# A turned tile of maxima takes its PSUM bank from another of two lists

## The chip, the cores and the metric

The kernel runs on one core of a Trainium2 chip. The metric is device time in microseconds (us); lower is better. The kernel before was run three times without the profiler: 1486.66, 1487.3 and 1488.96 us, median 1487.3. One further execution was profiled, and all rows quoted below come from that one.

## The reference

One transformer layer in its parallel form, float32, on 2048 rows of width 512: a layer norm, then attention with 32 heads of width 16 and a two-layer MLP of width 1792, both on the same normalised rows, and both added to the input.

```python
xn = _layernorm(x)
qkv = (xn @ wqkv).reshape(B, S, 3, H, Dh).transpose(2, 0, 3, 1, 4)      # S 2048, H 32, Dh 16
scores = jnp.einsum("bhqd,bhkd->bhqk", q, k) * Dh ** -0.5
p = jax.nn.softmax(scores, axis=-1)
o = jnp.einsum("bhqk,bhkd->bhqd", p, v).transpose(...).reshape(B, S, D) @ wo
h = jax.nn.gelu(jnp.einsum("bsd,df->bsf", xn, w1) + b1, approximate=True)
out = x + o + jnp.einsum("bsf,fd->bsd", h, w2) + b2
```

The softmax needs the largest score of each row before it can take exponents, and that maximum is where the change sits.

## The kernel before

**Blocks and units.** Attention is cut into 32 blocks (`t`): 8 groups of four heads times 4 stretches of 512 queries. A block has 16 units, so there are 512 units (`u`). In the unit loop (`unit`, line 745) two blocks are in work at once. Unit `u` computes the scores S of block `u // 16` for their maxima, four products of 128 queries by 512 keys, one for each head (`s_half`, line 366); VectorE (DVE) takes a row maximum of each (line 363, the tile `mt`). Unit `u` also computes, for `e = u - 19`, the transposed scores T (keys by queries; `e_half`, line 399), with the negative maximum already inside as extra rows of the operand `qst`, and ScalarE (ACT) takes the exponent of each (line 410, the tile `pe`). TensorE (PE) then multiplies the exponents by the values into a bank V (`v_half`, line 413).

**The order in a unit.** A unit has two slots, `a = 0` and `a = 1`. Written out, PE does: S of head 0, T of head 1, S of head 1, T of head 0, then a stretch of V products and of D products; then S of head 2, T of head 3, S of head 3, T of head 2, and V and D again. Below these are called S0, T1, S1, T0, S2, T3, S3, T2, and those of the next unit S0', T1' and so on. Each product is four matmuls of 32 columns, and uses one half (64 rows) of the PE array; S0 and T1, or V and D, run side by side in the two halves. "D" is all the other matrix work of the layer (projections, MLP, output projection), cut into groups and threaded through the units (`dense`, line 686): two to four products in a slot, by the group's pace. The order on every engine is the order in which the code is written; no scheduler changes it.

**The banks.** PSUM has eight banks, and four lists of them: S with banks 0, 1, 2; T with 3, 4, 5; D with 6; V with 7 (line 102). `banks(tag)` (line 107) takes the bank at the head of a list and puts it at the tail at once, so with three banks a product gets the bank that the product three before it in its list had. The matmul that first writes a bank waits until the last reader of that bank is done: a DVE maximum for an S bank, an ACT exponent for a T bank. When a D group ends, its bank goes to the tail of T's list and the next D group takes the head of that list (`dbank`, line 513; `Group.end`, line 550), so the T list always holds three banks while a D group is open, but one of the three may be a bank that D had until then. The finish of a D group reads it once, on ACT for most groups.

**The turn of the maxima.** After the last unit of a block, `s_end` (line 372) reduces `mt` to the block's negative maxima `mneg` (line 379) and leaves a closure `store` behind. It runs in the first unit of the next block, between the slots (line 783): two small matmuls by the identity turn `mneg` into a bank (line 386), DVE splits the turned tile into two float16 parts `mhl` (lines 389 and 390), and two DMAs write them out (line 393), from where four small DMAs (`m_rows`, line 345) bring them into the rows of `qst` that the block's T products read, three units later. There are 31 such turns in the unit loop, at units 32, 48, ..., 512; the turn of the first block is in the planned part before the loop, and has a bank of its own there.

Which reader the turn and the products behind it wait for follows from the lists. In 24 of the 31 turns no D group ended in the slot just before. In the other seven (units 64, 128, 256, 304, 336, 432 and 512) one did, and its bank has just gone to the tail of T's list.

Of the kernel before, what the change touches and what calls it, by code (L numbers as in the profile page):

```python
# [19 lines left out]
S = 2048  # L20
# [34 lines left out]
def layer_kernel(ctx: ExitStack, tc: tile.TileContext, x, wqkv, wo, w1, b1, w2, b2, out):  # L55
# [48 lines left out]
    def bank_tile(k, tag):  # L104
        return ps.tile([P, QB], F32, tag=f"B{k}", bufs=1, name="p" + tag)

    def banks(tag):
        k = free_banks[tag].pop(0)
        free_banks[tag].append(k)
        return bank_tile(k, tag)  # L110
# [48 lines left out]
    def given(engine, ns):  # L159
        backlog[engine] += ns  # L160
# [180 lines left out]
    def m_rows(t, h):  # L341
        g, qb = divmod(t, NQB)
        p, a = divmod(h, 2)
        dst = qst[g % 2][qb][64 * a + 62:64 * a + 64, p].rearrange("r (t q) -> r t q", q=P)
        nc.sync.dma_start(dst, m_d[t, 4 * h:4 * h + 4].rearrange("t r q -> r t q"))
# [26 lines left out]
    def s_end(u):  # L372

        t, i = divmod(u, 16)
        if i < 15:
            return
        g, qb = divmod(t, NQB)
        mneg = mnegs[t % 2]
        nc.vector.tensor_reduce(mneg[:, :16], mt_of[t].rearrange("p h t k -> p (h t) k"), axis=AX.X, op=ALU.max, negate=True)
        given("dve", 220)  # L380

        def store():

            pt = banks("S")
            for a in range(2):
                nc.tensor.matmul(pt[32 * a:32 * a + 32, :64], mneg[64 * a:64 * a + 64, :],
                                 ident[64 * a:64 * a + 64, 64 * a:64 * a + 64], start=True, stop=True)
            mhl = work.tile([64, 2, 64], F16, name="mhl", bufs=2)
            nc.vector.tensor_scalar_mul(mhl[:, 0], pt[:64, :64], 1.0 / MROW)
            nc.vector.scalar_tensor_tensor(mhl[:, 1], pt[:64, :64], 1.0 / MROW, mhl[:, 0], op0=ALU.mult, op1=ALU.subtract)  # L390
            given("dve", 300)
            for a in range(2):
                nc.sync.dma_start(m_d[t, :, :, 64 * a:64 * a + 64], mhl[32 * a:32 * a + 16])
            for h in range(4):
                m_rows(t, h)

        stores[t] = store
# [1097 lines left out]
```

## Time and profile before

| | |
|---|---|
| median of three runs | 1487.3 us |
| the profiled execution's own time | 1485.57 us |
| its span, first to last instruction | 1483.8 us |
| mean granted PE clock | 0.997 |
| turns of the maxima in the unit loop | 31, the first at 131.5 us, the last at 1415.1 us |

The profiled execution lies 1.7 us under the median of the runs, and 1.77 us of its time lie outside its span. In the rows, "pS", "pT", "pD" and "pV" are banks of the four lists, "gap" and "idle before" are idle time of the engine, and "62*32" names the part of the PE array in use. Rows of a timeline give start in us, length in us, engine, line, operation, tiles, and how many instructions were put together in the row; where several are put together, the length is from the start of the first to the end of the last. Ends of matmuls are modelled, so waits of PE are read from starts.

### The profile page before, as it was taken

Reading aid. Unit: us, or ns where it says so; the run is one execution under the profiler, and the core shown is the slowest. Engines: PE = TensorE matmul, PEld = TensorE weight load, DVE = VectorE, ACT = ScalarE, POOL = GpSimd, SP = SyncE. Lnnn points to the kernel's source line nnn. Section 1 sums busy time; section 2 is a strip of 40 time slices with the busy share of each in tenths; the row PEclk is TensorE's granted clock in tenths of the full one; section 3 lists DMA queues with packets and bytes.
Section 4 is the critical chain, followed back from the end, with each engine's and each line's share of the span. In section 5 each row is a group of like instructions: output and inputs, shape, how many; then the busy total and the mean of one; then the engine's idle time right before and its main releaser. Section 6 shows DMA issues by size and latency. Waiting matters only on the chain.

```text
span 1483.8 us, 88118 instructions
## 1 busy us (share of the span) xinstructions
PE 1467.1 (99%) x40158; PEld 811.5 (55%) x40158; DVE 1374.5 (93%) x2305; ACT 1259.2 (85%) x2366; POOL 662.2 (45%) x672
## 2 busy tenths in 40 slices
PE   8999999999999999999999999999999999999998
PEld 4445555555555555555555555555555555555554
DVE  7889999999999999999999999999999999999923
ACT  5868888888999888899988889998888998888884
POOL 3202857563787301377831037782115777121100
PEclk9999999999999999999999999999999999999999
DMA  6732556554224210221112111121112110111432
GB/s 213 226 113 70 163 171 195 160 157 144 76 72 114 65 37 23 68 62 41 44 43 87 30 36 44 53 73 44 43 38 80 50 37 21 56 55 31 141 93 95
DMA packets 112623, 124.83 MB, mean 84 GB/s; under 512 B 22908, under 2 KB 84220, under 8 KB 112248
## 3 DMA queue, kind: packets, MB, share of 16 engines
q1 hardware_dynamic: 112248, 119.18, 26.6%
q8 instruction: 314, 5.14, 1.5%
q14 instruction: 61, 0.50, 0.1%
HBM read 81.66 MB, written 37.34 MB: 80 GB/s over the span
## 4 chain that ended last, share of the span: by engine, by line
PE 89%; DVE 8%; ACT 1%; DMA 1%; issue 0%; SPq 0%; DVEq 0%; ACTq 0%
PE pV L169 26%; PE pD L169 25%; PE pS L169 18%; PE pT L169 18%; DVE mt L363 7%; PE pT L992 2%; DMA wq<-in_A_wqkv_dram 1%; PE pD L992 0%; DVE ac L1370 0%; ACT xs L945 0%; PE pT L962 0%; ACT xt L966 0%; DVE xt L975 0%; SPq L858 0%; DVE wvh L1075 0%
## 5 line engine op out<-in xcount | busy, mean ns | idle before, releaser
L363 DVE TENSOR_REDUCE mt<-pS 128x1 f32<-128x512 f32 x2029 | 1296.9, 684 | 44.0 <-PE pS L169 24.3
L410 ACT ACTIVATE pe<-pT 128x512 f32<-128x512 f32 x2048 | 1111.5, 599 | 178.0 <-PE pT L169 84.4
L169 PE MATMUL pV<-pe,vv 64*32 64x512 f32 x8192 | 1072.3, 594 | 0.1
L169 PE MATMUL pT<-qst,kst 64*32 64x512 f16 x8192 | 709.8, 378 | 0.5 <-issue 0.5
L169 PE MATMUL pS<-kst,qst 62*32 62x512 f16 x8116 | 614.3, 378 | 3.6 <-DVE mt L363 2.2
L169 PEld LDWEIGHTS <-qst 62*32 62x32 f16 x8192 | 283.6, 92 | 237.5 <-issue 58.0
L169 PE MATMUL pD<-xb,wc 64*32 64x512 f16 x5376 | 360.9, 377 | 0.0
L169 PEld LDWEIGHTS <-kst 64*32 64x32 f16 x8192 | 269.8, 91 | 159.9 <-issue 69.2
L169 PE MATMUL pD<-w_s,g 64*32 64x512 f16 x5376 | 356.4, 377 | 0.0
L169 PEld LDWEIGHTS pV<-pe,vv 64*32 64x32 f32 x8192 | 182.0, 105 | 88.9 <-PE pV L169 4.5
L169 PE MATMUL pD<-xt,wqk_h 64*32 64x512 f16 x2400 | 157.8, 378 | 0.0
L169 PEld LDWEIGHTS <-wc 64*32 64x32 f16 x5376 | 117.0, 91 | 43.0 <-issue 0.6
L169 PEld LDWEIGHTS <-g 64*32 64x32 f16 x5376 | 113.8, 92 | 41.0
L1337 POOL TENSOR_TENSOR xa<-xa,yt 128x512 f32<-128x512 f32 x16 | 20.4, 1278 | 232.0 <-ACT yt L1335 232.0
L466 POOL TENSOR_TENSOR osb<-osb,rb 128x512 f32<-128x512 f32 x31 | 39.8, 1283 | 165.8 <-DMA rb<-den_d 123.4
L1289 POOL TENSOR_TENSOR t<-hh 128x512 f32<-128x512 f32 x56 | 58.2, 1040 | 86.3 <-ACT hh L1312 85.3
L1291 POOL TENSOR_TENSOR t<-t,hh 128x512 f32<-128x512 f32 x56 | 71.7, 1281 | 4.7
L1284 POOL TENSOR_TENSOR t<-t,hh 128x512 f32<-128x512 f32 x56 | 71.7, 1281 | 4.7
L1283 POOL TENSOR_SCALAR t<-t,gs 128x512 f32<-128x512 f32 x56 | 38.7, 692 | 66.0 <-ACT t L1278 66.0
L1286 POOL TENSOR_TENSOR g<-t,g 128x512 f16<-128x512 f32 x56 | 65.2, 1163 | 4.7
L169 PEld LDWEIGHTS <-wqk_h 64*32 64x32 f16 x2400 | 54.5, 92 | 19.4 <-issue 1.4
L169 PE MATMUL pD<-wo_s,oc 64*32 64x512 f16 x828 | 54.7, 378 | 0.0
(160 smaller groups left out, 874.8 us busy)
## 6 DMA issues: line engine op xcount, KB each, us to landing
wc<-w_d SPq DMA_DIRECT2D x56, 256.0 KB
qk_d<-stg SPq DMA_DIRECT2D x32, 256.0 KB
rb<-den_d SPq DMA_DIRECT2D x124, 64.0 KB
wch<-in_B_w_dram SPq DMA_DIRECT2D x14, 512.0 KB
wch<-in_B_w_dram SPq DMA_DIRECT2D x28, 256.0 KB
w_d<-wsp SPq DMA_DIRECT2D x28, 256.0 KB
kst<-qk_d SPq DMA_DIRECT2D x64, 96.0 KB
qst<-qk_d SPq DMA_DIRECT2D x64, 96.0 KB
```

The costliest lines, as they stand in the source:

```text
L169: p = nc.tensor.matmul(*args, **kw)
L363: nc.vector.reduce_max(mt_of[t][:, n, qt, kb:kb + 1], s, axis=AX.X)
L410: nc.scalar.activation(pe, st, AF.Exp, scale=scale_of[g // 2])
L466: pooled((1280, lambda: nc.gpsimd.tensor_tensor(osb, osb, rb, op=ALU.mult)), (620, lambda: nc.gpsimd.tensor_scalar(ot[:, 0], osb, 1.0, 0.0 ...
L992: nc.tensor.matmul(tl[key], lhs, rhs, start=c + n == 0, stop=(c, n) == (NC - 1, 2))
L1283: pooled((690, lambda: nc.gpsimd.tensor_scalar(t1, t1, 1.0, gs[:, 1:2], op0=ALU.add, op1=ALU.mult)), (1280, lambda: nc.gpsimd.tensor_tenso ...
L1284: (1280, lambda: nc.gpsimd.tensor_tensor(t1, t1, hh, op=ALU.mult)),
L1286: (1160, lambda: nc.gpsimd.tensor_tensor(g[:, 1, f, :], t1, g[:, 0, f, :], op=ALU.subtract)),
L1289: pooled((1040, lambda: nc.gpsimd.tensor_tensor(t1, hh, hh, op=ALU.mult)), (620, lambda: nc.gpsimd.tensor_scalar(t1, t1, 1.0, 1.0 / GELU_A ...
L1291: (1280, lambda: nc.gpsimd.tensor_tensor(t1, t1, hh, op=ALU.mult)),
L1337: add = lambda: nc.gpsimd.tensor_tensor(xa, xa, yt, op=ALU.add)
```

## The change

The turn's tile is taken from the list T in place of the list S. Nothing else is edited.

```diff
@@ -381,7 +381,7 @@
 
         def store():
 
-            pt = banks("S")
+            pt = banks("T")
             for a in range(2):
                 nc.tensor.matmul(pt[32 * a:32 * a + 32, :64], mneg[64 * a:64 * a + 64, :],
                                  ident[64 * a:64 * a + 64, 64 * a:64 * a + 64], start=True, stop=True)
```

No instruction is added, removed or moved on any engine. What changes is which bank each product behind the turn gets, and so which engine it waits for. On PE at unit 32 this is the turn (line 386) and the first matmul of S2 behind it (`qst_2_89` is the query operand of the scores):

```order
-L386 MATMUL pS<-ident,mneg_101 32x64 [waits DVE_49,PE_49]
-L386 MATMUL pS<-ident,mneg_101 32x64
-L169 LDWEIGHTS qst_2_89
-L169 MATMUL pS<-kst_0_79,qst_2_89 32x512 [waits DVE_49]
+L386 MATMUL pT<-ident,mneg_101 32x64 [waits DVE_49,Activation_49]
+L386 MATMUL pT<-ident,mneg_101 32x64
+L169 LDWEIGHTS qst_2_89
+L169 MATMUL pS<-kst_0_79,qst_2_89 32x512
```

The turn now waits for an exponent on ACT as well as for `mneg` on DVE, and S2 behind it has no wait of its own left. At the start of the next unit on PE (the first matmul of S0' and of T1', whose weights are `qst_2_89` and `kst_3_82`) the wait for the two readers of the turned tile stands at another product:

```order
-L169 LDWEIGHTS qst_2_89 [waits DVE_49]
-L169 MATMUL pS<-kst_1_80,qst_2_89 32x512 [waits PE_49]
+L169 LDWEIGHTS qst_2_89
+L169 MATMUL pS<-kst_1_80,qst_2_89 32x512 [waits DVE_49]
```

```order
-L169 LDWEIGHTS kst_3_82
-L169 MATMUL pT<-qst_0_87,kst_3_82 32x512 [waits Activation_49]
+L169 LDWEIGHTS kst_3_82 [waits DVE_49]
+L169 MATMUL pT<-qst_0_87,kst_3_82 32x512 [waits PE_49]
```

S0' used to take the turn's bank and wait for `mhl`; now T1' does. Whose reader each product behind the turn waits for, from the lists (the seven turns are those with a D group just ended):

| product | 24 turns, before | 24 turns, after | 7 turns, before | 7 turns, after |
|---|---|---|---|---|
| turn | S3 of the unit before (DVE) | T2 of the unit before (ACT) | S3 of the unit before (DVE) | T1 (ACT) |
| S2 | S0 (DVE) | S3 of the unit before (DVE) | S0 (DVE) | S3 of the unit before (DVE) |
| T3 | T2 of the unit before (ACT) | T1 (ACT) | T1 (ACT) | T0 (ACT) |
| S3 | S1 (DVE) | S0 (DVE) | S1 (DVE) | S0 (DVE) |
| T2 | T1 (ACT) | T0 (ACT) | T0 (ACT) | the ended D group |
| S0' | the turn (DVE) | S1 (DVE) | the turn (DVE) | S1 (DVE) |
| S1' | S2 (DVE) | S2 (DVE) | S2 (DVE) | S2 (DVE) |
| T1' | T0 (ACT) | the turn (DVE) | the ended D group | the turn (DVE) |

In six of the seven turns the ended D group is read by ACT, at unit 512 by DVE, and there no S products are left. On ACT nothing moves; this is its order at the turn of unit 128, one of the seven, the same before and after (line 410 is the exponent, first of T1, then of T0, at the end of T3 and T2; line 1312 reads the bank of the ended D group):

```order
L410 ACTIVATE pe<-pT 128x512 [waits PE_49,Activation_49]
L410 ACTIVATE pe<-pT 128x512 [waits PE_49]
L207 TENSOR_LOAD fac_1704
L1312 ACTIVATE hh<-pD,b_s 128x512 [waits Pool_49]
L410 ACTIVATE pe<-pT 128x512 [waits PE_49] x2
```

The read of the D bank stands behind the exponent of T0 and ahead of those of T3 and T2.

## The prediction

> **What bounds the kernel now.** I read the page first: the span, the engines, the slices, the chain.
>
> ```profile
> span 1483.8 us, 88118 instructions
> PE 1467.1 (99%) x40158; PEld 811.5 (55%) x40158; DVE 1374.5 (93%) x2305; ACT 1259.2 (85%) x2366; POOL 662.2 (45%) x672
> PEclk9999999999999999999999999999999999999999
> PE 89%; DVE 8%; ACT 1%; DMA 1%; issue 0%; SPq 0%; DVEq 0%; ACTq 0%
> L169 PE MATMUL pS<-kst,qst 62*32 62x512 f16 x8116 | 614.3, 378 | 3.6 <-DVE mt L363 2.2
> ```
>
> PE is the bound, and 89% of the chain that ended last is PE, with the clock full in all slices. The last row seems to say that PE waits for maxima only 2.2 us in all. That is too little to trust: two matmul rows overlap in the two halves of the array, and ends are modelled, so a stall shows as idle only where both halves stand. I therefore read starts, on one turn in the middle of the run: PE, then DVE, then ACT in the timeline.
>
> ```profile
> 435.52 0.60 PE L169 MATMUL pD<-xb,wc 64*32 64x512 f16 x8
> 435.95 0.22 PE L386 MATMUL pS<-ident,mneg 64*32 64x64 f32 x2
> 436.06 0.38 PE L169 MATMUL pS<-kst,qst 62*32 62x512 f16 x1
> 436.11 0.40 PE L169 MATMUL pT<-qst,kst 64*32 64x512 f16 x3
> 436.55 0.40 PE L169 MATMUL pS<-kst,qst 62*32 62x512 f16 x4
> 436.57 0.40 PE L169 MATMUL pT<-qst,kst 64*32 64x512 f16 x4
> 436.77 0.40 PE L169 MATMUL pD<-xb,wc 64*32 64x512 f16 x4
> 436.79 0.60 PE L169 MATMUL pV<-pe,vv 64*32 64x512 f32 x4
> 437.63 0.39 PE L169 MATMUL pT<-qst,kst 64*32 64x512 f16 x2
> 437.87 0.42 PE L169 MATMUL pT<-qst,kst 64*32 64x512 f16 x4
> ...
> 435.08 0.22 DVE L379 TENSOR_REDUCE mneg<-mt 128x16 f32<-128x64 f32 x1
> 435.22 1.28 DVE L363 TENSOR_REDUCE mt<-pS 128x1 f32<-128x512 f32 x2
> 436.42 0.21 DVE L389 TENSOR_SCALAR mhl<-pS 64x64 f16<-64x64 f32 x1
> 436.66 0.22 DVE L390 SCALAR_TENSOR_TENSOR mhl<-pS,mhl 64x64 f16<-64x64 f32 x1
> 436.80 1.27 DVE L363 TENSOR_REDUCE mt<-pS 128x1 f32<-128x512 f32 x2
> ...
> 434.54 1.75 ACT L410 ACTIVATE pe<-pT 128x512 f32<-128x512 f32 x3
> 436.56 1.09 ACT L410 ACTIVATE pe<-pT 128x512 f32<-128x512 f32 x2 [0.27 <-PE pT L169]
> ```
>
> In the PE part, T1' and T0' (437.63, 437.87) stand 0.24 apart, V and D begin 0.22 after the pair ahead of them, 436.55 to 436.77: about 0.22 us is what a product takes in its half. Between the pair S2, T3 (436.06 to 436.11) and the pair S3, T2 (436.55, 436.57) lie 0.45 us or more, where 0.22 would do. The DVE part tells why: the maxima of S0 and S1 (435.22, 1.28 long) end at 436.50, and S3, which takes S1's bank, starts 0.05 us behind, at 436.55. DVE had 0.22 us for `mneg` ahead of them, and the turn has pushed S3 onto S1's bank. T2, written behind S3, waits with it, and then V and D. So at a turn PE stands for DVE; this is the only stall that the change can touch.
>
> **The change, part by part.** No instruction comes or goes, and durations stay. Three edges move.
>
> *S2, S3 and S0' each wait for one maximum earlier.* S3 then needs S0's maximum. The two maxima end 0.6 us apart (1.28 us for both against 0.684 mean in the group of line 363, below), so S0's ends at about 435.9 and holds S3 no longer; S3 could start 0.22 behind S2, near 436.3. As far as S goes, up to 0.27 us are freed.
>
> ```profile
> L363 DVE TENSOR_REDUCE mt<-pS 128x1 f32<-128x512 f32 x2029 | 1296.9, 684 | 44.0 <-PE pS L169 24.3
> ```
>
> *T3 and T2 each wait for one exponent later, in 24 turns.* The turn takes the bank of the unit before's T2, T3 that of T1, and T2 that of T0. The first ACT row above holds the exponents of T2 of the unit before, T1 and T0, the last ending at 436.29. With the same 0.05 us, T2 starts at 436.34 and not at 436.57. So the gain of this turn is 0.22 us and not 0.27: ACT is what is late next, not DVE. T3 needs T1's exponent, one before T0's, which is done before T3's place comes. V follows T2, and then T1'; all that is behind moves by the 0.22.
>
> I did the same sum at each of the 24 turns: T2's start, less the end of T0's exponent plus 0.05. In 17 it gives 0.20 to 0.25, together 3.9 us; in 7, where T1 and T0 came later, 0.09 to 0.13, together 0.7 us. One of the late ones, ACT and PE:
>
> ```profile
> 690.70 1.08 ACT L410 ACTIVATE pe<-pT 128x512 f32<-128x512 f32 x2 [0.18 <-PE pT L169]
> ...
> 691.93 0.40 PE L169 MATMUL pT<-qst,kst 64*32 64x512 f16 x4
> ```
>
> 691.78 plus 0.05 against 691.93: 0.10 us. The sum over the 24 is 4.6 us. From it I take 0.3: in four or five turns the D group of the slot is a slow one (three products, not four), S1' comes up sooner, and will wait for S2's maximum. In the turn shown that maximum ends near 437.47 (the second half of 436.80 + 1.27, less 0.6), and S1' starts beside T0', about 437.85, now, which leaves room for 0.33 us of gain; in the slow ones 0.13 less. That makes 4.3 us gained.
>
> *In six turns T2 waits for the D group that just ended.* There the list holds T1, T0 and D's old bank, the turn takes the first, T3 the second, T2 the third. ACT reads the D bank behind T0's exponent (three kinds of it: MLP hidden, projection, MLP output):
>
> ```profile
> 393.41 0.69 ACT L1312 ACTIVATE hh<-pD,b_s 128x512 f32<-128x512 f32 x1
> 393.82 0.40 PE L169 MATMUL pT<-qst,kst 64*32 64x512 f16 x4
> ...
> 220.00 0.62 ACT L604 ACTIVATE pf<-pD 128x512 f32<-128x512 f32 x1
> 220.19 0.40 PE L169 MATMUL pT<-qst,kst 64*32 64x512 f16 x4
> ...
> 860.77 0.60 ACT L1335 ACTIVATE yt<-pD 128x512 f32<-128x512 f32 x1
> 861.19 0.40 PE L169 MATMUL pT<-qst,kst 64*32 64x512 f16 x4
> ```
>
> The second row of each pair is T2 as it starts now. With the change it starts 0.05 behind the end of the first: 394.15 for 393.82, 0.33 lost; 220.67 for 220.19, 0.48; 861.42 for 861.19, 0.23 (0.25 without rounding). Four turns are of the first kind (0.33 to 0.36), one of the second, one of the third: 2.1 us. In these turns T3 also waits, for T0's exponent, some 0.35 us; it has that time, since S3 and T2 wait longer.
>
> *Is a late T2 late for both halves?* Here a rule can be weighed. An ordinary stretch:
>
> ```profile
> 440.03 0.61 PE L169 MATMUL pV<-pe,vv 64*32 64x512 f32 x4
> 440.09 0.39 PE L169 MATMUL pT<-qst,kst 64*32 64x512 f16 x4
> 440.30 0.55 PE L169 MATMUL pS<-kst,qst 62*32 62x512 f16 x8
> ```
>
> T1' starts at 440.09 though S0', written ahead of it, starts at 440.30 in the half that V still holds. So one half can run ahead of the other where no semaphore is open. The Trainium skill (PSUM — Partial Sum Buffer, section "Engine vs sequencer instructions") says that matmuls "start and complete in program order"; the starts here differ from it, and by it the six turns would lose all of 2.1 us on both halves, with nothing to win back. By the rows, what is lost in V's half (0.33) is only about half as much in D's (D starts at once when T2 is let go), and some may be made good where D has a product fewer than V needs. That bounds the loss between 1.1 and 2.1 us; V's half is the later one and the next V waits for both, so I take a value near the upper end, 1.8.
>
> *T1' waits for `mhl`.* Its second read ends at 436.66 + 0.22 = 436.88; T1' comes at 437.4 at the earliest. Nothing. *The last turn* has no S product to free; T3 moves behind T0's exponent and T2 stays there: 0 to 0.1 lost. *DMAs.* `mhl` is written when it was, while the T products that need its rows come 0.22 earlier. The closest case:
>
> ```profile
> 1246.80 2.42 SPq L393 DMA_DIRECT2D m_d<-mhl  x2
> 1250.77 1.14 SPq L345 DMA_DIRECT2D qst<-m_d  x4
> ...
> 1252.83 0.38 PE L169 MATMUL pT<-qst,kst 64*32 64x512 f16 x2
> ```
>
> The last small DMA is issued 0.92 us ahead of the first T, and that T needs only the second of the four; I take nothing, with 0.2 us in a few blocks as the other end.
>
> **Sum.** 4.3 gained, 1.8 lost: 2.5 us less. The profiled execution took 1485.57 us, and would take 1483.1; the median of runs lies 1.7 higher, so 1484.8 us. With the bounds (3.9 to 4.9 gained, 1.1 to 2.2 lost) this case runs from 1483.5 to 1485.6.
>
> **Rivals.** *The six turns cost nothing*, because the wait of T2 falls into time in which PE would stand anyway, and the 24 gain in full: 4.6 us, 1482.7. For it: T3 and S3 wait there as well, and halves run apart. Against: V follows T2 in the same half 0.22 behind it in all the rows above.
>
> *The wait moves to the maximum of S2.* DVE works without a break from 435.08 to 438.07 in the turn shown, 0.43 us of it for `mhl`. If S1' were held by S2's maximum in every turn, the gain would be given back there, and the six losses stay: 2.1 us slower, 1489.4. It decides where that maximum ends less than 0.05 ahead of S1'; the rows leave about 0.33 against a gain of 0.22, so only an order on DVE other than this one would do it. The Trainium skill (Perfetto Trace Analysis, section "Optimization Strategy") reads the same gap repeated on the busiest engine as a sign of too few PSUM buffers for the next tile; here the number of buffers stays the same, and the list is only chosen anew.
>
> *Nothing is saved*, since V of the next slots waits for exponents that ACT delivers no sooner: the second pair of exponents starts at 436.56 now and could start at about 436.5 at the soonest. Then 1487.3. Against: ACT has 15% idle.
>
> *The losses spread.* A late T2 makes its exponent late, ACT falls behind, and each of the six turns loses 1.3 us over several slots: 7.8 lost against 4.3, 1490.8. It would need ACT to be as full as PE; 85% busy speaks against it.
>
> **How the numbers follow.** About 0.2% (3 us) is what a measurement of this kernel can tell from no change, and my forecast lies just inside that. Chances: the forecast's case 0.56, about half of it on each side of the 3 us (0.28 faster, 0.28 within); the six turns free 0.19, all faster; the wait moved to S2's maximum 0.12, half within and half slower; nothing saved 0.06, within; spreading losses 0.07, slower by 0.06, within 0.01. Faster by over 0.2%: 0.47; within: 0.41; slower: 0.12. The range for 8 in 10 reaches from the free case, with 0.7 us for the spread of the runs shown, to a little above no change: 1482.0 to 1488.0.
>
> **What would show it right or wrong.** In the profile after, at the 24 turns: S3 about 0.2 us behind S2, no longer 0.05 behind S1's maximum, and T2 0.05 behind the end of T0's exponent. At units 64, 128, 256, 304, 336 and 432: T2 0.05 behind the end of ACT's read of the D bank, and V behind it late by 0.25 to 0.5. The times from one `mneg` to the next shorter by 0.1 to 0.25 us after the one kind and longer after the other. The forecast is wrong if S1' starts 0.05 behind S2's maximum in most turns, if V starts as late as before though T2 is earlier, or if a late T2 is still felt a unit further on.

## The result

The changed kernel took 1484.88 us (median of 21 runs, 1482.9 to 1488.41), the kernel before 1487.39 us (21 runs, 1483.81 to 1490.33). The ratio is 0.9984, with a 95% interval of 0.9977 to 0.9991: 2.4 us less (1.3 to 3.4). The profiled execution after took 1483.03 us.

The page of the kernel after, the same lines of it as were shown of before:

```profile
span 1481.3 us, 88125 instructions
PE 1465.3 (99%) x40158; PEld 812.2 (55%) x40158; DVE 1370.9 (93%) x2305; ACT 1259.3 (85%) x2366; POOL 662.2 (45%) x672
PEclk9999999999999999999999999999999999999999
PE 95%; DMA 1%; DVE 1%; ACT 1%; issue 0%; SPq 0%; DVEq 0%; ACTq 0%
L169 PE MATMUL pS<-kst,qst 62*32 62x512 f16 x8116 | 615.3, 378 | 1.4 <-DVE mt L363 1.4
```

DVE had 8% of the chain that ended last and has 1%; PE has 95%, and the idle time of PE ahead of S products, put down to maxima, went from 2.2 to 1.4 us. The page says which engine is no longer waited for, but not how much that is worth. That is read from starts again, at the turn of unit 144, the one shown before (PE, then DVE, then ACT, in the timeline of after; there its `mneg` started at 435.08, here at 435.31):

```profile
436.17 0.22 PE L386 MATMUL pT<-ident,mneg 64*32 64x64 f32 x2
436.18 0.38 PE L169 MATMUL pS<-kst,qst 62*32 62x512 f16 x3
...
436.38 0.55 PE L169 MATMUL pS<-kst,qst 62*32 62x512 f16 x2
436.57 0.37 PE L169 MATMUL pT<-qst,kst 64*32 64x512 f16 x1
...
436.61 0.54 PE L169 MATMUL pD<-xb,wc 64*32 64x512 f16 x2
436.78 0.59 PE L169 MATMUL pV<-pe,vv 64*32 64x512 f32 x1
...
437.48 0.53 PE L169 MATMUL pT<-qst,kst 64*32 64x512 f16 x2
...
437.74 0.50 PE L169 MATMUL pS<-kst,qst 62*32 62x512 f16 x3
437.87 0.38 PE L169 MATMUL pT<-qst,kst 64*32 64x512 f16 x1
...
435.31 0.22 DVE L379 TENSOR_REDUCE mneg<-mt 128x16 f32<-128x64 f32 x1
435.44 1.28 DVE L363 TENSOR_REDUCE mt<-pS 128x1 f32<-128x512 f32 x2
436.64 0.21 DVE L389 TENSOR_SCALAR mhl<-pT 64x64 f16<-64x64 f32 x1
436.88 0.22 DVE L390 SCALAR_TENSOR_TENSOR mhl<-pT,mhl 64x64 f16<-64x64 f32 x1
437.02 1.87 DVE L363 TENSOR_REDUCE mt<-pS 128x1 f32<-128x512 f32 x3
...
434.29 2.23 ACT L410 ACTIVATE pe<-pT 128x512 f32<-128x512 f32 x4
```

S3 starts at 436.38, 0.20 behind S2 (436.18); the maximum of S1 (435.44 + 1.28 = 436.72) would have held it till 436.77. T2 starts at 436.57, and T0's exponent, the last of the four, ends at 436.52: 0.05 between, as in all of the 24 turns. V follows at 436.78. T0' starts 2.56 us behind the start of `mneg` (437.87 less 435.31), where before it was 2.79 (437.87 less 435.08). So this turn gained 0.23 us.

The turn of unit 128, one of the six where T2 takes the bank of a D group that has just ended, in the timeline of after (PE, then ACT):

```profile
393.32 0.40 PE L169 MATMUL pT<-qst,kst 64*32 64x512 f16 x4
393.53 0.40 PE L169 MATMUL pS<-kst,qst 62*32 62x512 f16 x4
393.89 0.40 PE L169 MATMUL pT<-qst,kst 64*32 64x512 f16 x4
393.94 0.40 PE L169 MATMUL pD<-xb,wc 64*32 64x512 f16 x4
394.11 0.61 PE L169 MATMUL pV<-pe,vv 64*32 64x512 f32 x4
...
392.18 1.08 ACT L410 ACTIVATE pe<-pT 128x512 f32<-128x512 f32 x2 [0.28 <-PE pS L169]
393.15 0.69 ACT L1312 ACTIVATE hh<-pD,b_s 128x512 f32<-128x512 f32 x1
```

T3 starts 0.06 behind the end of T0's exponent (393.26), T2 0.05 behind the end of the read of the D bank (393.84), and V another 0.22 later. D, in the other half, starts 0.05 behind T2, although S3 ahead of it in its own half had started at 393.53 and a product takes about 0.22 there, so that the half was free at about 393.75. It is so in all six turns (0.04 to 0.05 behind T2): T2's wait holds what is written behind it in both halves.

For a sum over all turns I took the time from the first exponent of the turn's unit to the first exponent of the next unit (one unit on), and compared it with before, turn by turn. The 24 turns come to 4.68 us less, the six to 2.10 us more, the last turn to 0.01 more: 2.57 us less together. Taken two and three units on in place of one, the 24 stand at 4.67 and the six at 2.10 and 2.09: nothing is given back or won back later.

### The profile page after: what moved, and what is told of

Read it like the earlier page. It is cut to its first block, busy times and chain, and to the rows that moved or that the text cites. A ratio compares the mean times of both kernels' runs of the same rounds, so it can differ in the third digit from the quotient of the medians.

```text
span 1481.3 us, 88125 instructions
## 1 busy us (share of the span) xinstructions
PE 1465.3 (99%) x40158; PEld 812.2 (55%) x40158; DVE 1370.9 (93%) x2305; ACT 1259.3 (85%) x2366; POOL 662.2 (45%) x672
## 4 chain that ended last, share of the span: by engine, by line
PE 95%; DMA 1%; DVE 1%; ACT 1%; issue 0%; SPq 0%; DVEq 0%; ACTq 0%
PE pV L169 28%; PE pD L169 26%; PE pT L169 20%; PE pS L169 19%; PE pT L992 1%; DMA wq<-in_A_wqkv_dram 1%; PE pD L992 0%; DMA qk_d<-stg 0%; DVE ac L1370 0%; DMA kst<-qk_d 0%; ACT xs L945 0%; DVE mt L363 0%; ACT wqk_h L881 0%; DVE xt L975 0%; PE pT L962 0%
## 5 line engine op out<-in xcount | busy, mean ns | idle before, releaser
L169 PEld LDWEIGHTS <-kst 64*32 64x32 f16 x8192 | 274.3, 91 | 162.6 <-issue 71.5
```

Of the source, the lines that this page charges most:

```text
L169: p = nc.tensor.matmul(*args, **kw)
```

## The experiments

The edits of the first four runs are shown against the kernel before, the others against what is named there. Sums by turn are worked out as above, one unit on if nothing else is said, against the profile of before. A ratio with its interval is that of the record and not the quotient of the two medians; the two differ by up to 0.0007.

### The 24 turns alone

```diff
-            pt = banks("S")
+            pt = banks("S" if t in (3, 7, 15, 18, 20, 26, 31) else "T")
```

> The turn takes its bank from T only where no D group has just ended (24 turns), and from S in the other seven. My theory: the 24 turns gain 4.7 us in all (T2 then waits for the exponent of T0, 0.09 to 0.25 us sooner than it now waits for the maximum of S1), and the six costly ones lose nothing: about 4.7 us under the kernel before, ratio 0.9969. Rival (the six turns cost nothing on the whole, what they lose is won back later): no more is gained than by the change itself, ratio 0.9984.

Measured: 1484.4 us (5 runs) against 1488.83, ratio 0.9965 (0.9951 to 0.9979). The interval holds the 0.9969 expected and not the rival's 0.9984. The 24 turns gave 4.67 us, the six 0.00. In the timeline of this kernel at unit 128, T2 (the second row) starts long before the read of the D bank (the first) is over:

```profile
394.46 0.69 ACT L1312 ACTIVATE hh<-pD,b_s 128x512 f32<-128x512 f32 x1
...
394.88 0.40 PE L169 MATMUL pT<-qst,kst 64*32 64x512 f16 x4
```

So the two terms of the sum are apart, and the losing one can be left out by the choice of the list.

### The seven turns alone

```diff
-            pt = banks("S")
+            pt = banks("T" if t in (3, 7, 15, 18, 20, 26, 31) else "S")
```

> The turn takes its bank from T only in the seven turns where a D group has just ended, and from S in the other 24. My theory: T2 waits for ACT's read of the D bank, 0.24 to 0.5 us later than now, 2.1 to 2.4 us in all: ratio 1.0015. Rival (what is lost in those slots is won back): ratio 1.0000.

Measured: 1489.27 us against 1488.83, ratio 1.0007 (0.9997 to 1.0017). The interval holds what both theories expect, so the time doesn't decide. The trace does: the six turns lose 2.11 us one unit on, and 2.10 and 2.09 two and three units on; the 24 come to 0.00. At unit 128, in the timeline of this kernel:

```profile
395.78 0.69 ACT L1312 ACTIVATE hh<-pD,b_s 128x512 f32<-128x512 f32 x1
...
396.53 0.40 PE L169 MATMUL pT<-qst,kst 64*32 64x512 f16 x4
396.57 0.40 PE L169 MATMUL pD<-xb,wc 64*32 64x512 f16 x4
396.74 0.61 PE L169 MATMUL pV<-pe,vv 64*32 64x512 f32 x4
```

T2 waits for the end of that read (395.78 + 0.69 = 396.47) and V for T2. The loss is real at its place and stays.

### The turn in T, and one bank of S skipped

S3 gets S1's bank again, as before the change, while T's list stays as after it.

```diff
-            pt = banks("S")
+            pt = banks("T")
+            free_banks["S"].append(free_banks["S"].pop(0))
```

> The turn takes a bank of T as in the change, and S's list is turned on by one bank besides, unused, so that S2, S3 and S0' wait for the same maxima as before. My theory: the gain of the 24 turns is S3's earlier maximum and nothing else, so S3 is back at 0.05 us behind S1's maximum and the 24 turns gain nothing, while the six lose their 2.1 us: ratio 1.0015. Rival (it is the turn's own presence among the score banks, its wait or its DVE reads of a score bank, that costs): the 24 still gain, ratio 0.9984.

Measured: 1490.78 us against 1488.83, ratio 1.0006 (0.9997 to 1.0016). The interval shuts out the rival's 0.9984. The 24 turns give 0.13 us more instead of 4.68 less; the six lose 2.09, where the change lost 2.10. At unit 144, in the timeline of this kernel (PE, then DVE):

```profile
442.78 0.40 PE L169 MATMUL pS<-kst,qst 62*32 62x512 f16 x4
442.80 0.40 PE L169 MATMUL pT<-qst,kst 64*32 64x512 f16 x4
...
443.02 0.60 PE L169 MATMUL pV<-pe,vv 64*32 64x512 f32 x4
...
441.45 1.28 DVE L363 TENSOR_REDUCE mt<-pS 128x1 f32<-128x512 f32 x2
```

S3 stands 0.05 behind S1's maximum (442.73) again, T2 0.02 behind S3, and the gain is gone. The skipped bank gives S2 and S0' back their old readers too, but neither was held by them: S2 starts 0.87 to 0.88 us behind the start of `mneg` with the turn in S as with the turn in T (435.96 less 435.08, 436.18 less 435.31), and the turn's last read ends at 436.88 in before, S0' starts at 437.65. So the whole gain is S3's earlier maximum, and the whole loss is T2's wait in the T list; neither depends on the other.

### No bank at all: the maxima turned by DVE

If a bank for the turn costs a wait whichever list it comes from, a turn without PE and PSUM should cost none. DVE turns the tile in blocks of 32 by 32 in SBUF, the split works on 128 partitions, and `mhl` goes out in four DMAs. The diff shows the main lines; besides them the turn's bank is no longer taken, and the tile of `mhl` is laid out anew, with room for the turned maxima `tr`.

```diff
-            for a in range(2):
-                nc.tensor.matmul(pt[32 * a:32 * a + 32, :64], mneg[64 * a:64 * a + 64, :],
-                                  ident[64 * a:64 * a + 64, 64 * a:64 * a + 64], start=True, stop=True)
+            nc.vector.transpose(tr, mneg)
...
-            for a in range(2):
-                nc.sync.dma_start(m_d[t, :, :, 64 * a:64 * a + 64], mhl[32 * a:32 * a + 16])
+            for a in range(4):
+                nc.sync.dma_start(m_d[t, :, :, 32 * a:32 * a + 32], mhl[32 * a:32 * a + 16])
```

> The maxima are turned on DVE, 32 by 32 blocks from SBUF to SBUF, with no matmul and no bank; the split is done on 128 by 32, and four DMAs write it out in place of two. My theory (the turn's whole excess over an ordinary unit, some 0.33 us, is waits for banks and the two matmuls): S3 waits for S0's maximum and T2 for T1's exponent, both early, and 6 to 10 us are gained, ratio 0.993 to 0.996, less what DVE's longer work takes back at S1'. Rival (DVE is the bound in the turn, and any list only moves the wait): ratio 0.997 or more. The four DMAs may make the first T product of a block wait.

Measured: 1510.1 us (4 runs) against 1488.83, ratio 1.0141 (1.0126 to 1.0157), a clear miss, 21 us slower. A part of the theory did come: in the 30 turns ahead of the last, the first exponent of the next unit, that of T1', comes 10.6 us sooner in all than before. But two units on the sum stands at 4.1 us more than before, and three units on at 18.6. The waits of PE in before (first) and in this kernel; columns are us in total, times, and the longest:

```profile
PE pS L169 <- DVE mt L363: 2.2, 6, 1.4
```

```profile
PE pS L169 <- DVE mt L363: 11.2, 19, 1.4
PE pT L169 <- DMA qst<-m_d: 8.8, 12, 1.6
```

Two new waits, 9.0 and 8.8 us, make up most of the 21. The second has mostly to do with SP. The issues at the turn of unit 144 in the timelines of before and of this kernel:

```profile
436.90 1.24 SPq L393 DMA_DIRECT2D m_d<-mhl  x2
439.31 1.15 SPq L345 DMA_DIRECT2D qst<-m_d  x4
```

```profile
446.71 2.50 SPq L391 DMA_DIRECT2D m_d<-mhl  x4
450.38 1.15 SPq L345 DMA_DIRECT2D qst<-m_d  x4
```

Four issues take 2.50 us where two took 1.24. `mneg` started at 435.08 and 443.84, so the reads into `qst` are issued 6.54 us behind it and no longer 4.23. Of these 2.31 us, 1.26 are the longer issue; 1.05 stand ahead of it, because the split was late at this turn. Over the 31 turns the reads are issued 1.8 us later on the average, 1.2 of it by the issue and 0.5 by the split. In 12 blocks the first T products then come before the rows do (not in the one shown); in these 12 the time from the last write's issue to the first read's is 0.9 us longer as well, and why isn't shown.

The first comes from DVE, at some turns only. The timeline of this kernel, DVE and POOL, then PE:

```profile
445.17 0.20 DVE L386 STREAM_TRANSPOSE mhl<-mneg 128x32 f32<-128x32 f32 x1
445.41 0.18 DVE L387 TENSOR_SCALAR mhl<-mhl 128x32 f16<-128x32 f32 x1
445.63 1.05 DVE L388 SCALAR_TENSOR_TENSOR mhl<-mhl 128x32 f16<-128x32 f32 x1
446.60 0.68 DVE L363 TENSOR_REDUCE mt<-pS 128x1 f32<-128x512 f32 x1
...
445.47 1.17 POOL L466 TENSOR_TENSOR ot<-osb,ot 128x512 f16<-128x512 f32 x1
...
447.34 0.40 PE L169 MATMUL pS<-kst,qst 62*32 62x512 f16 x4 [0.93 <-DVE mt L363]
```

The subtraction of the split took 1.05 us here and 0.19 in most turns. It ends at 446.68, POOL's instruction at 446.64. Of the 62 instructions of the split in the 31 turns, 17 took 0.36 to 1.29 us, and every one of the 17 ended 36 to 51 ns behind a POOL instruction that had begun before it. The others took 0.18 to 0.21 us. In the kernels before and after, which read the turned tile from PSUM, none took longer than 0.22, though in each kernel 26 of the 62 ran with a POOL instruction in progress from their start to their end. So with its operands in SBUF the split waits for POOL, and PE then waits for the maxima behind it. The Trainium skill (SBUF — State Buffer, section "Who interferes with whom") states that a VectorE instruction with two SBUF inputs contends with a GpSimd instruction that reads SBUF, that one in a two-port mode, such as a `tensor_scalar` can enter, contends with GpSimd too, and that the one issued first holds the shared ports for its whole length while the other blocks. The 17 agree: in each the POOL instruction had begun first.

### T2 behind V and D in the turns' units

With the turn in T, what holds V is T2 ahead of it in its half. Here T2 is written behind the slot's V and D products in the turns' units (the edit is against the changed kernel).

```diff
-                if 0 <= e < NU:
+                if 0 <= e < NU and not (b == 3 and u % 16 == 0 and u > 16):
                     e_half(e, b ^ 1)
...
+                if a == 1 and 0 <= e < NU and u % 16 == 0 and u > 16:
+                    e_half(e, 2)
```

> The turn's bank stays in T; in the units of the turns alone, T2 is written behind the slot's V and D products and no longer ahead of them. My theory (what a turn costs is that V stands behind T2 in its half, and T2 behind an exponent or behind ACT's read of the ended D bank): V then starts behind T3 and S3 alone. The 24 turns gain 0.28 to 0.33 us against before instead of 0.1 to 0.25, and the six turns, where T2's bank comes free 1.8 to 2.2 us after mneg and T2's new place is at about 2.0, lose 0 to 0.1 instead of 0.24 to 0.48: about 7 us less than before, a ratio of 0.995. Rival 1 (S2's maximum, which already ends 0.05 us ahead of S1' in most turns after the change, sets the unit once T2 is out of the way): the 24 turns stay at 4.7 and only the six come to about 0, ratio 0.997. Rival 2 (T2's exponent, 0.5 us later, makes ACT late and the V products two slots on wait): slower than the changed kernel, 0.999 to 1.002.

Measured: 1483.76 us against 1487.13, ratio 0.9979 (0.997 to 0.9988); the 0.995 of my theory lies outside. Taken two units on (one unit on, T2's late exponent stands ahead of the exponent that ends the measure), the six turns come to 0.31 us less than before instead of 2.10 more, where my theory had 0 to 0.1 each more, but the 24 only to 3.38 less. Three units on it is 0.22 and 3.23. My 0.28 to 0.33 a turn stands in 6 of the 24. Rival 1 (0.997) is nearer, yet its reason isn't what took the gain in the worst turns: seven turns (units 48, 96, 144, 224, 352, 400, 496) gave next to nothing, 0.06 less to 0.08 more, and in each the first D product of the next slot started 0.05 us behind the end of T2's exponent. In the timeline of this kernel at unit 400 (PE, then ACT):

```profile
1117.33 1.04 PE L169 MATMUL pV<-pe,vv 64*32 64x512 f32 x8
1117.85 0.83 PE L169 MATMUL pD<-xb,wc 64*32 64x512 f16 x12
...
1117.21 1.57 ACT L410 ACTIVATE pe<-pT 128x512 f32<-128x512 f32 x3 [0.57 <-PE pT L169]
```

The first of these three exponents is T2's; at 0.59 us it ends at 1117.80. D begins at 1117.85, 0.52 behind V. There a D group opens, and takes the T bank whose last reader is T2's exponent. Why most of the other turns gain no more than with T2 at its old place isn't settled. S1' stands 0.05 behind S2's maximum in them, but it does so in all of the 24, also in the six that gained more, so this alone doesn't tell them apart.

### The same, with S in the seven turns of the ended groups

The two edits together (T2 late in all turns, the turn's bank as in the run of the 24 alone).

> As the run with T2 behind V and D, but the seven turns with an ended D group take the turn's bank from S as before the change. There S3 waits for S1's maximum again (0.25 us) and T2 for T0's exponent, which is long done at T2's new place. If V was held only by T2, these six turns gain as well, by up to 0.25 us each where S3 stands in the other half than V: 1 to 1.5 us less than with T in all turns, ratio 0.994. If S3's wait holds V too, they gain nothing, and the two kernels are alike within 0.3 us (ratio 0.995). By rival 1, 0.9965 to 0.997, as with 24 turns in T and T2 at its old place.

Measured: 1483.94 us against 1487.13, ratio 0.9981 (0.9972 to 0.999). None of the ratios expected lies inside: they were built on the expectation of the run above. By turn, two units on, the six give 0.28 us, the 24 3.27. That is the second of the two ways expected: the six turns gain nothing beside the run above (0.31). With T2 out of the way it makes no difference to their sum which list the turn takes; single turns differ by up to 0.2 us, either way.

### T2 late only where no D group opens

```diff
+    def late(u):
+        return u % 16 == 0 and 16 < u < 512 and u not in (48, 96, 144, 224, 352, 400, 496)
...
-                if 0 <= e < NU and not (b == 3 and u % 16 == 0 and u > 16):
+                if 0 <= e < NU and not (b == 3 and late(u)):
...
-                if a == 1 and 0 <= e < NU and u % 16 == 0 and u > 16:
+                if a == 1 and 0 <= e < NU and late(u):
                     e_half(e, 2)
```

(against the kernel with T2 late in all turns)

> As the run with T2 behind V and D, but T2 keeps its old place at unit 512 and in the seven turns (units 48, 96, 144, 224, 352, 400, 496) where, with T2 late, the first D product of the next slot started 0.05 us behind the end of T2's exponent. There a D group opens and takes the T bank whose last reader is that exponent. If that is why these turns gained nothing (they came to +0.06 to -0.06 us instead of -0.16 to -0.25), then these seven gain 1.6 us together again, the other 17 gain 3.6, the six with an ended D group 0.3: 5.4 us less than before in the unit loop, a ratio of 0.9963, the best so far. Rival (a late T2 makes the whole ACT queue late and the loss only happened to show there): the sum in the loop stays at 3 to 4 us, ratio 0.9975.

Measured: 1483.91 us against 1488.75, ratio 0.9969 (0.9956 to 0.9982). The interval holds both ratios expected, so the time doesn't decide. By turn, two units on: the seven give 1.58 us, the other 17 3.45, the six 0.31, 5.33 in all before rounding (5.13 three units on), where 5.4 was expected and the rival had 3 to 4. At unit 400, in its timeline:

```profile
1116.48 0.61 PE L169 MATMUL pV<-pe,vv 64*32 64x512 f32 x4
1116.57 0.61 PE L169 MATMUL pD<-xb,wc 64*32 64x512 f16 x8
```

D begins 0.09 behind V. The seven turns were picked from the run above; with T2 back at its old place in these alone the gain is back in all seven (0.21 to 0.25 each), so what held them was T2's late exponent, and the order of the list says through which bank. The ratio lies beside that of the 24 turns alone (0.9965); the two kernels weren't timed against each other, and by time they can't be told apart. Both are faster than the kernel before, and by the sums over their turns (4.67 and 5.33 against 2.57) than the change as made.

## Why the prediction was right

The forecast was 1484.8 us, the measured median 1484.88. That they agree to 0.1 us is luck: the interval of the ratio leaves 1.3 to 3.4 us, and two misses below cancel. The mechanism is what stands. Step by step:

| step | forecast, us | in the trace after, us |
|---|---|---|
| 24 turns | -4.3 (-4.6 before a deduction of 0.3) | -4.68 |
| six turns, T2 behind the D bank's read | +1.8 (+2.1 in full) | +2.10 |
| last turn | 0 to +0.1 | +0.01 |
| net | -2.5 | -2.57 |

- **S3 waits for one maximum earlier, and T0's exponent is late next.** Right in both parts: S3 stands 0.2 behind S2, T2 0.05 behind the end of T0's exponent. One reading was off, at no cost to the sum: 436.06 is the last of S2's four matmuls in before, the first three start at 435.96, so S3 without its wait would have come at about 436.16 and not 436.3. T0's exponent, which lets T2 go at 436.34, is later than either. By turn the gain is 0.21 to 0.25 us in 17 and 0.09 to 0.14 in seven, as worked out from the rows of before. The run with one bank of S skipped shows that it hangs on S3's maximum alone.
- **The deduction of 0.3** for the turns with a slow D group was not there. It supposed that S1', held by S2's maximum, would hold the unit.
- **The six turns.** The place and the wait were right; the size was taken too low. T2's 0.24 to 0.48 us are lost in full. I had reckoned that D's half, which loses less, would make some of it good. It does lose less (at unit 128, D starts 0.18 later behind `mneg`, V 0.32), but V's half sets the unit, and nothing is made good three units on. The two misses, 0.4 and 0.3, are of opposite sign, which helped the net. The rule weighed there (the Trainium skill, PSUM — Partial Sum Buffer, section "Engine vs sequencer instructions") gave 2.1, and 2.10 came. At T2's wait the trace agrees with it, since D in the other half stands behind T2 too; in the ordinary stretch of the prediction it doesn't. Which of the two sets the 2.10 isn't separated: V's place behind T2 in its own half gives the same, and the run with T2 behind V took both away.
- **T1' and `mhl`, the DMAs.** Nothing in the sum, as forecast: at unit 144 the second read of the turned tile ends at 437.10 and T1' starts at 437.48, and no matmul waits for the rows of maxima (one weight load does, for 0.29 us, at 1336.07). But the margin isn't there everywhere: at unit 496 the slot has only one D product, the read ends at 1372.41 and T1' starts 0.05 behind it. That turn gained its 0.21 us all the same.
- **The rivals.** That the six turns cost nothing is excluded by the 2.10, that nothing is saved by the 4.68, that losses spread by the sums two and three units on. A wait for S2's maximum does appear, but gives nothing back (next point).
- **The sign that misled.** I wrote that the forecast would be wrong if S1' started 0.05 behind S2's maximum in most turns. It does, in all of the 24 (before in one): in the turn above the first of the last three maxima ends near 437.69 (437.02 + 1.87 less twice 0.6), and S1' starts at 437.74. Yet it starts 2.43 us behind `mneg`, where it was about 2.77 before, and T0' and V behind it are 0.22 to 0.23 earlier. A wait that is there need not be the one that sets the unit; the sign should have been T0', not S1'.

What a single profile can't show is the net. Its span fell by 2.5 us, but 0.87 of that stands ahead of the first exponent of the loop (95.727 against 94.854), where nothing was changed, and about as much (0.9) is lost again in the units without a turn, in steps of up to 0.35 us of both signs. The sum over the turns agrees with the ratio of the runs (2.57 against 2.4); that the span agrees is luck.

## What to carry to other kernels

A tile that borrows a bank shifts every product behind it in that list by one reader, so list whose reader each product gets before and after, and compare the end of that reader, plus the release measured in the trace, with the product's start. Look at the places where the list's order differs from the usual one (here a D group that ends or opens): they gave back 2.1 of 4.7 us, and a choice by place keeps the 4.7. When a product is delayed to get it out of the way, ask who takes its bank next.

## What was not expected of the hardware

The split of the maxima on DVE, with its operands in SBUF, waited for POOL in 17 of 62 cases, for up to 1.1 us, and ended 36 to 51 ns behind the POOL instruction; with the turned tile in PSUM it took at most 0.22 us in all turns.

In an ordinary stretch the two halves of the array did not start their matmuls in the written order (440.09 for T1', 440.30 for S0', written ahead of it, in before). Yet a product that waited for a bank held the half that it doesn't use as well: in the six turns D started 0.04 to 0.05 us behind T2, at unit 128 some 0.19 us after its half was free.

Some of the difference between the profiled executions of two kernels stands in the same stretch, in the units without a turn between 37 and 95, as waits that the profile puts down to "issue", with nothing waited for that it shows. PE's waits from 130 to 320 us, in the run with one bank of S skipped and in the kernel after; in before there are none:

```profile
PE pD L169 <- issue: 1.5, 2, 0.8
PE pS L169 <- issue: 1.1, 1, 1.1
```

```profile
PE pD L169 <- issue: 0.2, 1, 0.2
```

What PE waits for there stays open.
